# Products of masked scores and v in 64x64 tiles, a second copy of v, and another order of all steps

## The chip, the cores and the metric

The kernel runs on one core of one Trainium2 chip. The core has a matrix engine (TensorE, PE in the rows; PEld is its weight load), VectorE (DVE), ScalarE (ACT), GpSimd (POOL), and a sync engine (SP) whose queue issues all transfers. The metric is the device time of one execution in microseconds: before the change 369.61 us, the median of three runs (367.24 to 371.17).

## The reference

Inputs are q, k, v and f_logit of 4 batches, 8 heads, 768 positions and 48 channels. The first half is a gated linear recurrence for every head, the second a position mixing with a rotation and a channel mixing:

```python
f = 1.0 / (1.0 + np.exp(-f_logit))
for t in range(S):
    state = f[:, :, t, :, None] * state + np.einsum('bhd,bhe->bhde', k[:, :, t], v[:, :, t])
    y[:, :, t] = np.einsum('bhd,bhde->bhe', q[:, :, t], state)
x = y.transpose(0, 2, 1, 3).reshape(B, S, 384)
theta = x @ w_theta
zr, zi = x * np.cos(theta), x * np.sin(theta)
u = x + np.einsum('ts,bsd->btd', w_tok_r, zr) + np.einsum('ts,bsd->btd', w_tok_i, zi)
out = u + np.maximum(u @ w_ch, 0.0)
```

## The kernel before

The recurrence runs in 24 chunks of 128 positions, six for each batch. Gates become running sums of logarithms, q and k are scaled by them, and a chunk is then plain matrix work. q and k hold two heads in the partitions: of pair p (four of them) head 2p lies in rows 0 to 47 and head 2p+1 in rows 64 to 111. j is the head of the pair, t the half of the chunk (64 positions each).

The last chunk of a batch is taken whole (`whole_chunk`, 4 of 24). The other 20 go by halves, so that scores are needed only within a half:

- `sc` (L295): scores, k by q, 48 rows and 64 columns. The rows that a product reads follow from j, and its output lies in the rows of half t; the two heads write two PSUM banks.
- `ma` (L306): VectorE multiplies the scores by the causal mask, one instruction for each bank.
- `ke`, `kt`, `up` (L312, L324): k is turned and multiplied with v into the new state of either half; `sa`, `st`, `sm` add and fade the state.
- `ou` (L354, L361): L354 is the old state by q, and L361 the masked scores by v. The scores of one head lie in all 128 rows (half 0 above, half 1 below), so L361 loads 128 rows of weights, and v is kept with zeros in the rows of the other half: `vs[m]` has the two copies t = 0, 1, in two buffers `vz` that GpSimd fills with zeros at the start and mends after a whole chunk (L527).

A program matmul in fp32 takes two passes and stands as two MATMUL rows in the trace: L361 has 24 x 16 x 2 = 768.

After that `xc`, `xt`, `xs` bring the result to x and turn it, `th` (L405) are the angles, `tn`, `se`, `ab`, `tr`, `ro`, `zh`, `zl` the cosine, the sine and the split in two parts. `f` (L461) is one piece of the position mixing; there are 8 groups (batch and half of the output) of 18 pieces. `c` (L479) is the channel mixing, `cv` (L493) its end, and `so` the store.

The four engines run what the table `ORDER` names, in that order: each word is a step, taken the next time for the next chunk (or piece), and /A, /D or /P puts it on ScalarE, VectorE or GpSimd. SP's queue is issued in the order in which the loads become due in the same table (`lf`, `lk`, `lq`, `lv`; `lw` is a part of the weights, which arrive as 64-bit numbers and are decoded by `d1`, `d2`, `d3`). Of the pool `a`, which all of the recurrence uses, there are four PSUM banks.

Of the kernel before, what the change touches and what calls it, by code (L numbers as in the profile page):

```python
# [8 lines left out]
F32 = mybir.dt.float32  # L9
# [3 lines left out]
ALU = mybir.AluOpType  # L13
# [4 lines left out]
B, H, S, D = 4, 8, 768, 48  # L18
DM = H * D
P = 128  # L20
NP = H // 2
C = 128
NC = S // C
# [65 lines left out]
def gla_moe_kernel(  # L89
# [5 lines left out]
    v: bass.AP,  # L95
    vt: bass.AP,
# [6 lines left out]
    nc = tc.nc  # L103

    const = ctx.enter_context(tc.tile_pool(name="const", bufs=1))
    sb = ctx.enter_context(tc.tile_pool(name="sb", bufs=1))
# [25 lines left out]

    vz = [const.tile([P, 2, DM], F32, tag=f"v{i}", name=f"v{i}") for i in range(2)]
    for i in range(2):
        nc.gpsimd.memset(vz[i], 0.0)
# [95 lines left out]
    loaded, ps_, phased, vs = {}, {}, {}, {}  # L231
# [41 lines left out]

    pss, scs, psks, kts, pkvs, mids, states, pys, xs, pxts = ({} for _ in range(10))
    HALVES = [(t, slice(64 * t, 64 * t + 64)) for t in range(2)]

    def whole_chunk(m):
        return m % NC == NC - 1

    def bank(shape, name):  # L280
        return ps.tile(shape, F32, tag="a", bufs=4, name=name)

    def att_scores(m):
        kt, qt = loaded["k", m], loaded["q", m]
        pss[m] = [bank([P, NP, C], f"pss{m}{j}") for j in range(2)]
        for p in range(NP):
            if whole_chunk(m):
                for j in range(2):
                    r = slice(64 * j, 64 * j + D)
                    nc.tensor.matmul(pss[m][j][:, p, :], kt[r, p, :], qt[r, p, :], start=True, stop=True)  # L290
            else:
                for t, ts in HALVES:
                    for j in range(2):
                        r = slice(64 * j, 64 * j + D)
                        nc.tensor.matmul(pss[m][j][ts, p, :64], kt[r, p, ts], qt[r, p, ts], start=True, stop=True)  # L295

    def att_mask(m):
        if whole_chunk(m):
            w, mask = C, causal
            scs[m] = [sb.tile([P, NP, C], F32, tag="sc", bufs=2, name=f"sc{m}{j}") for j in range(2)]  # L300
        else:
            w, mask = C // 2, causal_h
            t = sb.tile([P, 2, NP, C // 2], F32, tag="sc", bufs=2, name=f"sc{m}")
            scs[m] = [t[:, j] for j in range(2)]
        for j in range(2):
            nc.vector.tensor_tensor(scs[m][j], pss[m][j][:, :, :w],  # L306
                                    mask.unsqueeze(1).to_broadcast([P, NP, w]), op=ALU.mult)
# [10 lines left out]
    def att_state(m):  # L318
        pkvs[m] = [bank([P, NP, D], f"pkv{m}{t}") for t in range(2)]
        for p in range(NP):  # L320
            for j, r in HALVES:
                h = 2 * p + j
                for t, ts in HALVES:
                    nc.tensor.matmul(pkvs[m][t][r, p, :], kts[m][ts, p, r], vs[m][ts, t, h * D:(h + 1) * D],  # L324
                                     start=True, stop=True)
# [16 lines left out]
    def att_out(m):  # L342
        qt, sc = loaded["q", m], scs[m]
# [13 lines left out]
        for p in range(NP):  # L357
            for j in range(2):
                h = 2 * p + j
                for t, ts in HALVES:  # L360
                    nc.tensor.matmul(pys[m][j][ts, p, :], sc[j][:, p, ts if whole_chunk(m) else slice(0, 64)],  # L361
                                     vs[m][:, 0 if whole_chunk(m) else t, h * D:(h + 1) * D],
                                     start=(old[t] is None and p == 0), stop=(p == NP - 1))
# [157 lines left out]
    def load_v(m):  # L521
        vs[m] = vz[m % 2]
        if whole_chunk(m):
            nc.sync.dma_start(vs[m][:, 0, :], v[m // NC, m % NC])
        else:
            if m > 1 and whole_chunk(m - 2):
                nc.gpsimd.memset(vs[m][64:, 0, :], 0.0)  # L527
            for t, ts in HALVES:
                nc.sync.dma_start(vs[m][ts, t, :], v[m // NC, m % NC, ts])
# [16 lines left out]
    def group(fn):  # L546
# [9 lines left out]
        "lv": load_v, "lw": load_part,  # L556
# [104 lines left out]
def layout(inputs):  # L661
    import numpy as np

    def rows(a):
# [11 lines left out]
        "v": np.ascontiguousarray(v.transpose(0, 2, 1, 3).reshape(B, NC, C, DM)),  # L676
        "vt": np.ascontiguousarray(vt),
# [25 lines left out]
```

## Time and profile before

| | |
|---|---|
| median of three runs | 369.61 us |
| the profiled execution | 370.48 us |
| its span | 368.7 us |
| mean granted clock of TensorE | 0.989 |
| PE busy | 341.1 us (93%) |
| DVE busy | 278.4 us (76%) |
| ACT busy | 195.0 us (53%) |
| POOL busy | 81.9 us (22%) |
| bytes moved | 40.82 MB |

The profile is of one execution. Its span goes from the first to the last instruction; the 1.8 us between the span and the execution's time lie outside the program's instructions. Busy times of one engine are unions, so instructions that overlap on one engine count once; mean durations are of single instructions. A row of the timeline merges neighbouring instructions of one line, and its second number reaches from the first start to the last end.

### The profile page before, as it was taken

The numbers are of one execution on the slowest core, as the hardware profiler recorded it, in microseconds if no ns is written. First come the engines' busy times: TensorE is split into PE (matmuls) and PEld (weight loads), VectorE is DVE, ScalarE is ACT, GpSimd is POOL, SyncE is SP. The second block draws the span as 40 slices with busy tenths as digits, with TensorE's granted clock in tenths as the row PEclk, the third lists the DMA queues.
The fourth block names the chain that finished last, engine by engine and source line by source line (L and its number), as shares of the span: only waits on it lengthen the run. The fifth ranks groups of instructions, "written<-read, shape, count | busy, mean of one in ns | idle before, by whom it ended". The sixth has DMA issues, their size and how long they took to land.

```text
span 368.7 us, 9853 instructions
## 1 busy us (share of the span) xinstructions
PE 341.1 (93%) x4176; PEld 295.3 (80%) x4176; DVE 278.4 (76%) x471; ACT 195.0 (53%) x326; POOL 81.9 (22%) x79
## 2 busy tenths in 40 slices
PE   0399799999998999999999999999999999999992
PEld 0386476655886679888999999989989999999992
DVE  4799998999779999998798997887775577304131
ACT  6599878554747938898856597346300335000000
POOL 4542610023832154651113430000100000000000
PEclk9999899999999999999999999999999999999997
DMA  7989789500443333324345432241100100010002
GB/s 264 349 279 349 229 260 331 170 2 15 125 148 109 108 92 80 98 75 128 97 134 151 129 98 58 73 115 30 34 23 23 44 0 2 21 43 2 22 23 92
DMA packets 21970, 40.82 MB, mean 111 GB/s; under 512 B 2720, under 2 KB 8864, under 8 KB 21920
## 3 DMA queue, kind: packets, MB, share of 16 engines
q1 hardware_dynamic: 21920, 40.12, 34.7%
q8 instruction: 35, 0.57, 0.7%
q14 instruction: 15, 0.12, 0.1%
HBM read 35.39 MB, written 4.72 MB: 109 GB/s over the span
## 4 chain that ended last, share of the span: by engine, by line
PE 64%; DVE 20%; DMA 6%; ACT 4%; issue 3%; POOL 1%; SPq 0%; DVEq 0%; ACTq 0%; POOLq 0%
PE pm L461 36%; PE pch L479 9%; PE pth L405 6%; PE py L361 3%; DVE f L249 3%; DVE k L269 2%; PE pss L295 2%; DMA f<-in_f_dram 2%; PE py L354 2%; PE pkv L324 2%; DMA raw<-in_w_i_dram 2%; PE psk L312 2%; DVE sc L306 1%; PE pxt L374 1%; DVE uhl L472 1%
## 5 line engine op out<-in xcount | busy, mean ns | idle before, releaser
L461 PE MATMUL pm<-wp,z 128*128 128x384 f32 x648 | 122.5, 340 | 0.0
L461 PEld LDWEIGHTS pm<-wp,z 128*128 128x128 f32 x648 | 111.6, 188 | 1.3
L461 PE MATMUL pm<-value,z 128*128 128x384 f32 x144 | 50.9, 501 | 0.4 <-DVE z L438 0.4
L479 PE MATMUL pch<-uhl,wch 128*128 128x384 f32 x216 | 41.9, 342 | 0.0
L461 PEld LDWEIGHTS pm<-value,z 128*128 128x128 f32 x144 | 26.7, 194 | 17.0 <-DVE z L438 0.8
L479 PEld LDWEIGHTS pch<-uhl,wch 128*128 128x128 f32 x216 | 37.1, 188 | 1.0 <-DVE ut L493 0.4
L249 DVE TENSOR_TENSOR_SCAN f<-carry,f 128x512 f32<-128x512 f32 x24 | 30.3, 1273 | 1.3 <-ACT f L245 1.3
L465 DVE TENSOR_TENSOR ut<-pm,ut 128x384 f32<-128x384 f32 x24 | 12.9, 553 | 23.6 <-PE pm L461 23.4
L239 POOL TENSOR_SCALAR f<-f 128x512 f32<-128x512 f32 x14 | 24.1, 1723 | 27.1 <-DMA f<-in_f_dram 23.9
L264 POOL TENSOR_TENSOR q<-q,p 128x512 f32<-128x512 f32 x15 | 22.5, 1500 | 29.4 <-DMA q<-in_q_dram 21.9
L260 POOL COPY pes<-p 128x4 f32<-128x4 f32 x24 | 10.9, 454 | 78.2 <-ACT p L256 78.1
L361 PE MATMUL py<-v,sc 128*64 128x48 f32 x768 | 28.1, 228 | 0.0
L256 ACT ACTIVATE p<-f 128x512 f32<-128x512 f32 x24 | 15.1, 630 | 23.4 <-DVE q L264 12.7
L295 PE MATMUL pss<-q,k 48*64 48x64 f32 x640 | 15.6, 234 | 12.7 <-DVE k L269 11.0
L146 ACT CAST uhl<-ut 128x384 fp32r<-128x384 f32 x14 | 6.9, 506 | 37.9 <-DVE ut L465 37.8
L361 PEld LDWEIGHTS py<-v,sc 128*64 128x64 f32 x768 | 25.1, 141 | 1.3
L493 DVE SCALAR_TENSOR_TENSOR ut<-pch,ut 128x384 f32<-128x384 f32 x24 | 13.2, 552 | 15.9 <-PE pch L479 15.8
L295 PEld LDWEIGHTS pss<-q,k 48*64 48x64 f32 x640 | 12.6, 142 | 15.6 <-DVE k L269 11.0
L405 PE MATMUL pth<-wth,xh 128*128 128x384 f32 x108 | 22.5, 343 | 1.0 <-DVE xh L146 0.8
L421 ACT ACTIVATE w<-w 128x384 f32<-128x384 f32 x22 | 11.5, 523 | 21.1 <-DVE w L416 21.1
L445 DVE TENSOR_TENSOR z<-w,z 128x768 fp32r<-128x768 f32 x18 | 18.3, 1019 | 4.2 <-ACT z L146 3.9
L324 PEld LDWEIGHTS pkv<-v,ktok 64*64 64x64 f32 x640 | 12.7, 142 | 10.2 <-issue 7.2
(87 smaller groups left out, 602.9 us busy)
## 6 DMA issues: line engine op xcount, KB each, us to landing
f<-in_f_dram SPq DMA_DIRECT2D x24, 256.0 KB, 2.8
q<-in_q_dram SPq DMA_DIRECT2D x24, 256.0 KB, 3.1
k<-in_k_dram SPq DMA_DIRECT2D x24, 256.0 KB, 3.4
raw<-in_w_r_dram SPq DMA_DIRECT2D x12, 384.0 KB, 5.0
raw<-in_w_i_dram SPq DMA_DIRECT2D x12, 384.0 KB, 5.6
out_dram<-ut SPq DMA_DIRECT2D x24, 192.0 KB, 2.0
v<-in_v_dram SPq DMA_DIRECT2D x40, 96.0 KB, 3.5
raw<-in_w_theta_dram SPq DMA_DIRECT2D x3, 384.0 KB, 5.8
```

Source lines behind the costliest of these rows:

```text
L239: on(nc.vector).tensor_scalar(ft, ft, F_MIN, None, op0=ALU.max)
L249: nc.vector.tensor_tensor_scan(fl, carry[:, pairs(h)].rearrange("p n t -> p (n t)"), fl, 0.0, ALU.mult, ALU.add)
L256: nc.scalar.activation(ps_[m][:, pairs(h)], ft, AF.Exp, scale=-1.0)
L264: on(nc.vector).tensor_tensor(qt, qt, ps_[m][:, pairs(h)], op=ALU.mult)
L295: nc.tensor.matmul(pss[m][j][ts, p, :64], kt[r, p, ts], qt[r, p, ts], start=True, stop=True)
L324: nc.tensor.matmul(pkvs[m][t][r, p, :], kts[m][ts, p, r], vs[m][ts, t, h * D:(h + 1) * D], start=True, stop=True)
L361: nc.tensor.matmul(pys[m][j][ts, p, :], sc[j][:, p, ts if whole_chunk(m) else slice(0, 64)], vs[m][:, 0 if whole_chunk(m) else t, h * D:(h ...
L405: nc.tensor.matmul(pths[m], l, r, start=(n == 0), stop=(n == len(ms) - 1))
L445: nc.vector.tensor_tensor(zs[m][:, 0], ws[m], zs[m][:, 1], op=ALU.subtract)
L461: nc.tensor.matmul(pms[g, d], l, r, start=(s == 0 and i == 0), stop=(s == NC - 1 and i == len(ms) - 1))
L479: nc.tensor.matmul(pcs[g, d], l, r, start=(es[0] == 0 and n == 0), stop=(es[-1] == KD - 1 and n == len(ms) - 1))
L493: nc.vector.scalar_tensor_tensor(u, pcs[g, d], 0.0, u, op0=ALU.max, op1=ALU.add)
```

## The change

The weights of L361 become 64 rows: the scores of head j are written to the rows of row tile j (both halves of the chunk side by side in the free dimension, one bank for both heads), the mask is applied in one instruction, and v comes a second time, by heads (`v_heads`, prepared outside the kernel), so that row tile j also holds v of head j for both halves. The state's update reads a plain copy of v. The buffers with zeros, their memsets and the two half loads go; a load `lz` comes in. In `ou` the loop over t is now outside the loop over j, in the whole chunks too. `ORDER` is written anew in all lines.

```diff
 ORDER = (
-    "lf lf lf lq gc lq go gc/P lq gc lk lk go gs lk lv go gs lv lw ge gs gq gp ge gk lw sc gk gq/P lf lf ke",
...
+    "lf lf lf lv lv gc/P lq lq gc/P gc go lq lz lz lk go gs lk lk go gs lw ge gs gq gp lw ge gk sc lf gk gq/P",
...
-    vz = [const.tile([P, 2, DM], F32, tag=f"v{i}", name=f"v{i}") for i in range(2)]
-    for i in range(2):
-        nc.gpsimd.memset(vz[i], 0.0)
...
     def att_scores(m):
         kt, qt = loaded["k", m], loaded["q", m]
-        pss[m] = [bank([P, NP, C], f"pss{m}{j}") for j in range(2)]
-        for p in range(NP):
-            if whole_chunk(m):
+        if whole_chunk(m):
+            pss[m] = [bank([P, NP, C], f"pss{m}{j}") for j in range(2)]
+            for p in range(NP):
                 for j in range(2):
                     r = slice(64 * j, 64 * j + D)
                     nc.tensor.matmul(pss[m][j][:, p, :], kt[r, p, :], qt[r, p, :], start=True, stop=True)
-            else:
+        else:
+            pss[m] = bank([P, NP, 2, 64], f"pss{m}")
+            for p in range(NP):
                 for t, ts in HALVES:
-                    for j in range(2):
+                    for j, js in HALVES:
                         r = slice(64 * j, 64 * j + D)
-                        nc.tensor.matmul(pss[m][j][ts, p, :64], kt[r, p, ts], qt[r, p, ts], start=True, stop=True)
+                        nc.tensor.matmul(pss[m][js, p, t, :], kt[r, p, ts], qt[r, p, ts], start=True, stop=True)
...
+            scs[m] = sb.tile([P, NP, 2, 64], F32, tag="sc", bufs=2, name=f"sc{m}")
+            nc.vector.tensor_tensor(scs[m].rearrange("s p t q -> s (p t) q"), pss[m].rearrange("s p t q -> s (p t) q"),
+                                    causal_h.unsqueeze(1).to_broadcast([P, 2 * NP, 64]), op=ALU.mult)
...
         for p in range(NP):
-            for j in range(2):
-                h = 2 * p + j
-                for t, ts in HALVES:
-                    nc.tensor.matmul(pys[m][j][ts, p, :], sc[j][:, p, ts if whole_chunk(m) else slice(0, 64)],
-                                     vs[m][:, 0 if whole_chunk(m) else t, h * D:(h + 1) * D],
-                                     start=(old[t] is None and p == 0), stop=(p == NP - 1))
+            for t, ts in HALVES:
+                for j, js in HALVES:
+                    if whole_chunk(m):
+                        h = 2 * p + j
+                        l, r = sc[j][:, p, ts], vs[m][:, h * D:(h + 1) * D]
+                    else:
+                        l, r = sc[js, p, t, :], vhs[m][js, t, p, :]
+                    nc.tensor.matmul(pys[m][j][ts, p, :], l, r, start=(old[t] is None and p == 0), stop=(p == NP - 1))
...
     def load_v(m):
-        vs[m] = vz[m % 2]
-        if whole_chunk(m):
-            nc.sync.dma_start(vs[m][:, 0, :], v[m // NC, m % NC])
-        else:
-            if m > 1 and whole_chunk(m - 2):
-                nc.gpsimd.memset(vs[m][64:, 0, :], 0.0)
-            for t, ts in HALVES:
-                nc.sync.dma_start(vs[m][ts, t, :], v[m // NC, m % NC, ts])
+        vs[m] = sb.tile([P, DM], F32, tag="v", bufs=2, name=f"v{m}")
+        nc.sync.dma_start(vs[m], v[m // NC, m % NC])
+
+    def load_vh(m):
+        vhs[m] = sb.tile([P, 2, NP, D], F32, tag="vh", bufs=2, name=f"vh{m}")
+        nc.sync.dma_start(vhs[m], v_heads[m // NC, m % NC])
```

Two places show how the built program's order moves. The first is TensorE in chunk 1, from the old state's products to the scores of chunk 2 (st0 and mid1 are the states of the two halves, py10 and py11 the outputs of the two heads, sc1 the masked scores). Before:

```order
L354 MATMUL py10_363<-st0_231,q1_107 64x48
L354 MATMUL py11_364<-st0_231,q1_107 64x48
L354 MATMUL py10_363<-mid1_358,q1_107 64x48
L354 MATMUL py11_364<-mid1_358,q1_107 64x48
...
L361 MATMUL py10_363<-v1_86,sc1_304 64x48 x2
L361 MATMUL py11_364<-v1_86,sc1_304 64x48 x2
...
L295 MATMUL pss20_412<-q2_113,k2_123 64x64
L295 MATMUL pss21_413<-q2_113,k2_123 64x64
```

And now:

```order
L352 MATMUL py10_355<-st0_235,q1_107 64x48
L352 MATMUL py11_356<-st0_235,q1_107 64x48
L352 MATMUL py10_355<-mid1_335,q1_107 64x48
L352 MATMUL py11_356<-mid1_335,q1_107 64x48
...
L363 MATMUL py10_355<-vh1_118,sc1_318 64x48
L363 MATMUL py11_356<-vh1_118,sc1_318 64x48
...
L295 MATMUL pss2_395<-q2_114,k2_127 64x64 x16
L322 MATMUL pkv20_428<-v2_285,ktok2_341 64x48
```

The products of scores and v now alternate between the heads as the old state's do, the 16 score products write one tile, and the state's update (L322) of chunk 2 follows them directly, where before a transposition stood between the two.

The second place is the start of SP's queue, from the third load of q to the first of the mixing weights (raw2; raw0 and raw1 are w_theta). Before:

```order
L518 DMA q2_113<-in_q_dram 128x512
L518 DMA k0_116<-in_k_dram 128x512
L518 DMA k1_118<-in_k_dram 128x512
L518 DMA k2_123<-in_k_dram 128x512
L172 DMA raw0_132<-in_w_theta_dram 128x768
L529 DMA v0_85<-in_v_dram 64x384 x2
L529 DMA v1_86<-in_v_dram 64x384 x2
L172 DMA raw0_132<-in_w_theta_dram 128x768
L172 DMA raw1_145<-in_w_theta_dram 128x768
L172 DMA raw2_180<-in_w_r_dram 128x768
```

And now:

```order
L518 DMA f2_98<-in_f_dram 128x512
L523 DMA v0_100<-in_v_dram 128x384
L523 DMA v1_102<-in_v_dram 128x384
L518 DMA q0_105<-in_q_dram 128x512
L518 DMA q1_107<-in_q_dram 128x512
L518 DMA q2_114<-in_q_dram 128x512
L527 DMA vh0_116<-in_v_heads_dram 128x384
L527 DMA vh1_118<-in_v_heads_dram 128x384
L518 DMA k0_120<-in_k_dram 128x512
L518 DMA k1_125<-in_k_dram 128x512
L518 DMA k2_127<-in_k_dram 128x512
L169 DMA raw0_132<-in_w_theta_dram 128x768 x2
```

The first k, which was the seventh transfer, is now the eleventh, behind two loads of v and two of its copy by heads.

## Rows read from the trace of the kernel before

**Rows 1.** Stretches: us, then PE, PEld, DVE, ACT, POOL busy, clock, DMA share, GB/s.

```profile
0.00:73.00 73.00, 54.82 (x815) 38.52 (x816) 62.55 (x98) 55.49 (x95) 23.66 (x29) 0.98 0.85 282
10.00:20.00 10.00, 5.15 (x86) 4.17 (x86) 7.62 (x13) 5.57 (x9) 6.03 (x5) 1.00 1.05 354
100.00:160.00 60.00, 58.32 (x886) 47.44 (x885) 56.34 (x88) 42.95 (x74) 27.13 (x21) 1.00 0.34 102
220.00:369.00 149.00, 141.93 (x1426) 137.26 (x1424) 83.10 (x158) 37.56 (x65) 2.27 (x4) 0.98 0.12 37
```

**Rows 2.** What TensorE waited for from 73 us on: total us, times, longest.

```profile
PE pth L405 <- DVE xh L146: 0.8, 1, 0.8
PE pkv L324 <- DMA v<-in_v_dram: 0.7, 1, 0.7
PE pkv L324 <- DVE sc L306: 0.4, 1, 0.4
...
PE pss L295 <- DVE w L416: 0.2, 1, 0.2
```

**Rows 3.** Timeline of TensorE at 73 us: start, us, engine, line, operation.

```profile
72.93 3.39 PE L461 MATMUL pm<-value,z 128*128 128x384 f32 x10
```

**Rows 4.** The chain of waits: its last piece, and one at 48 us.

```profile
48.83 6.50 DMA raw<-in_w_i_dram
...
361.97 0.56 DVE ut L493
```

**Rows 5.** Timeline of TensorE: merged bursts of L354 in one chunk, first and last.

```profile
255.65 0.23 PE L354 MATMUL py<-st,q 48*64 48x48 f32 x2
255.66 0.23 PE L354 MATMUL py<-mid,q 48*64 48x48 f32 x2
...
255.94 0.22 PE L354 MATMUL py<-st,q 48*64 48x48 f32 x2
```

**Rows 6.** Timeline of TensorE, 166 to 169 us: the products of a batch's first chunk.

```profile
166.65 0.67 PE L354 MATMUL py<-mid,q 48*64 48x48 f32 x16
167.24 1.14 PE L361 MATMUL py<-v,sc 128*64 128x48 f32 x32
168.31 0.69 PE L295 MATMUL pss<-q,k 48*64 48x64 f32 x32
168.94 0.45 PE L461 MATMUL pm<-wp,z 128*128 128x384 f32 x1
```

**Rows 7.** Timeline of TensorE, 192 to 194 us: scores and state's update back to back.

```profile
192.85 0.69 PE L295 MATMUL pss<-q,k 48*64 48x64 f32 x32
193.37 0.63 PE L324 MATMUL pkv<-v,ktok 64*64 64x48 f32 x32
```

**Rows 8.** Groups of VectorE: busy us, mean ns, idle before and its releaser.

```profile
L306 DVE TENSOR_TENSOR sc<-pss,causal_h 128x256 f32<-128x256 f32 x40 | 15.0, 416 | 4.7 <-PE pss L295 4.5
L306 DVE TENSOR_TENSOR sc<-pss,causal 128x512 f32<-128x512 f32 x8 | 5.1, 683 | 0.3 <-PE pss L290 0.3
L239 DVE TENSOR_SCALAR f<-f 128x512 f32<-128x512 f32 x10 | 6.7, 668 | 3.7 <-DMA f<-in_f_dram 3.6
L264 DVE TENSOR_TENSOR q<-q,p 128x512 f32<-128x512 f32 x9 | 6.1, 682 | 0.0
L185 DVE TENSOR_SCALAR raw<-raw 128x768 int32<-128x768 int32 (+1 forms) x16 | 9.2, 586 | 1.3 <-DMA raw<-in_w_theta_dram 1.3
L195 DVE SCALAR_TENSOR_TENSOR raw<-raw 128x768 int32<-128x768 int32 (+1 forms) x16 | 14.4, 901 | 0.0
L196 DVE SCALAR_TENSOR_TENSOR value<-raw 128x768 int32<-128x768 int32 (+1 forms) x14 | 14.0, 1000 | 0.5
```

**Rows 9.** Transfers: count, KB each, median us from issue to landing.

```profile
f<-in_f_dram SPq DMA_DIRECT2D x24, 256.0 KB, 2.8
raw<-in_w_r_dram SPq DMA_DIRECT2D x12, 384.0 KB, 5.0
v<-in_v_dram SPq DMA_DIRECT2D x4, 192.0 KB, 3.3
```

More of the change, by code (lines that the diff above doesn't have):

```diff
@@ L95, in gla_moe_kernel @@
     v: bass.AP,
+    v_heads: bass.AP,
     vt: bass.AP,
@@ L229, in gate_tables @@
             nc.scalar.preload_act_table_set(GATE_SET)
-    loaded, ps_, phased, vs = {}, {}, {}, {}
+    loaded, ps_, vs, vhs = {}, {}, {}, {}
     def pairs(h):
@@ L290, in att_scores @@
                     nc.tensor.matmul(pss[m][j][:, p, :], kt[r, p, :], qt[r, p, :], start=True, stop=True)
-            else:
+        else:
+            pss[m] = bank([P, NP, 2, 64], f"pss{m}")
+            for p in range(NP):
                 for t, ts in HALVES:
-                    for j in range(2):
+                    for j, js in HALVES:
                         r = slice(64 * j, 64 * j + D)
-                        nc.tensor.matmul(pss[m][j][ts, p, :64], kt[r, p, ts], qt[r, p, ts], start=True, stop=True)
+                        nc.tensor.matmul(pss[m][js, p, t, :], kt[r, p, ts], qt[r, p, ts], start=True, stop=True)
     def att_mask(m):
         if whole_chunk(m):
-            w, mask = C, causal
             scs[m] = [sb.tile([P, NP, C], F32, tag="sc", bufs=2, name=f"sc{m}{j}") for j in range(2)]
-        else:
-            w, mask = C // 2, causal_h
-            t = sb.tile([P, 2, NP, C // 2], F32, tag="sc", bufs=2, name=f"sc{m}")
-            scs[m] = [t[:, j] for j in range(2)]
-        for j in range(2):
-            nc.vector.tensor_tensor(scs[m][j], pss[m][j][:, :, :w],
-                                    mask.unsqueeze(1).to_broadcast([P, NP, w]), op=ALU.mult)
+            for j in range(2):
+                nc.vector.tensor_tensor(scs[m][j], pss[m][j], causal.unsqueeze(1).to_broadcast([P, NP, C]), op=ALU.mult)
+        else:
+            scs[m] = sb.tile([P, NP, 2, 64], F32, tag="sc", bufs=2, name=f"sc{m}")
+            nc.vector.tensor_tensor(scs[m].rearrange("s p t q -> s (p t) q"), pss[m].rearrange("s p t q -> s (p t) q"),
+                                    causal_h.unsqueeze(1).to_broadcast([P, 2 * NP, 64]), op=ALU.mult)
     def att_keys(m):
@@ L323, in att_state @@
                 for t, ts in HALVES:
-                    nc.tensor.matmul(pkvs[m][t][r, p, :], kts[m][ts, p, r], vs[m][ts, t, h * D:(h + 1) * D],
+                    nc.tensor.matmul(pkvs[m][t][r, p, :], kts[m][ts, p, r], vs[m][ts, h * D:(h + 1) * D],
                                      start=True, stop=True)
@@ L357, in att_out @@
         for p in range(NP):
-            for j in range(2):
-                h = 2 * p + j
-                for t, ts in HALVES:
-                    nc.tensor.matmul(pys[m][j][ts, p, :], sc[j][:, p, ts if whole_chunk(m) else slice(0, 64)],
-                                     vs[m][:, 0 if whole_chunk(m) else t, h * D:(h + 1) * D],
-                                     start=(old[t] is None and p == 0), stop=(p == NP - 1))
+            for t, ts in HALVES:
[6 more added lines that the diff above has]
+                    nc.tensor.matmul(pys[m][j][ts, p, :], l, r, start=(old[t] is None and p == 0), stop=(p == NP - 1))
     def att_x(m):
@@ L555, in gla_moe_kernel @@
     fn |= {
-        "lv": load_v, "lw": load_part,
+        "lv": load_v, "lz": inner(load_vh), "lw": load_part,
         "d1": decode_low, "d2": decode_high, "d3": decode_join, "d4": split_hi,
@@ L676, in layout @@
         "v": np.ascontiguousarray(v.transpose(0, 2, 1, 3).reshape(B, NC, C, DM)),
+        "v_heads": np.ascontiguousarray(v.reshape(B, NP, 2, NC, 2, 64, D).transpose(0, 3, 2, 5, 4, 1, 6)
+                                        .reshape(B, NC, P, 2, NP, D)),
         "vt": np.ascontiguousarray(vt),
```

66 rows, old and new, of the table ORDER are left out of this document.

## The prediction

> **What bounds the kernel now.** I read the busy time by stretch first. In the first 73 us [rows 1] VectorE is busy for 62.55 us, the transfers for 0.85 of the time at 282 GB/s, and TensorE for 54.82 us. After that TensorE is hardly ever idle: 58.32 of 60 us at 100 to 160 us, and in the last stretch all but the tail. The list of what TensorE waited for from 73 us on [rows 2] adds up to 2.6 us in six waits of 0.8 to 0.2 us. So there are two parts. The **front** ends where the tenth piece of the position mixing (f9) starts a run of such pieces, at 72.9 us [rows 3]; it is paced by VectorE and the transfers, and in places by both, since the chain of waits runs through a weight's landing of 6.50 us [rows 4]. The **rest**, 289 us up to the end of TensorE's work at 362.0 us [rows 4], goes at TensorE's own pace, and what lies there is worth what it costs TensorE. Counted from the two tables of steps, the blocks ahead of f9 are the same set before and after: chunks 0 to 5 with their angles, and nine pieces. So the rest holds the same blocks too, with 15 of the 20 chunks that go by halves.
>
> How long the small products take is read from the timeline. In the old state's products [rows 5] the rows come in bursts of four (two of st, two of mid: two heads by two halves, so four tiles of the array), and five bursts later, from 255.65 to 255.94 us, the clock has gone 0.29 us: a **round of 0.058 us**. A first chunk has only one half there, hence two tiles, and its 16 rows take 167.24 - 166.65 = 0.59 us [rows 6], as much as 32 rows in four tiles (scores, 168.94 - 168.31 = 0.63 us). The round stays at its length; what counts is how many different tiles it holds. L361 loads all 128 rows, so only the two halves of the columns are apart: 32 rows in 168.31 - 167.24 = 1.07 us.
>
> **The change part by part**, for the rest (15 chunks) where nothing else is said.
>
> *Products of scores and v.* With 64 rows of weights, alternating over heads and halves, they are in four tiles like the old state's: 8 rounds in place of 16, so 8 x 0.058 = 0.46 us less in a chunk, 7.0 us in 15.
>
> *Scores.* Their output now lies in the rows of their own head, so head 0 goes from row tile 0 to column tile 0 and head 1 from 1 to 1, for both halves. Two tiles of four are used, where before all four were. The nearest row is the first chunk's old state with two tiles [rows 6]: 16 rounds in place of 8, 0.46 us more in a chunk, **7.0 us in 15**. The two terms cancel. Bounds for the scores: no cost (four to a round as now), or single file (32 rounds, 1.9 us in place of 0.46). I take two to a round, since this alternation of two row tiles is the one that the row of 16 shows.
>
> *Changes of the tile's shape.* Scores followed directly by the state's update, both 64x64, start 193.37 - 192.85 = 0.52 us apart [rows 7]; scores followed by 128x128 work 0.63 us [rows 6]. A change of shape thus costs 0.11 us. Before, each `ou` goes from 64x64 to 128x64; now it stays, and often the next scores or update does too. Over both tables I count 134 changes of shape before and 93 after; in the rest 99 and 73. 26 x 0.11 = **2.9 us less**. Bounds: nothing, and 26 x 0.14 = 3.7 us (0.14 is L361's 1.07 less its 16 rounds).
>
> *Whole chunks.* In the products the column halves now come t0, t0, t1, t1 and no longer in turn. Neighbours in different tiles remain (second and third, fourth and next first), so I take nothing; the other end is one tile to a round in the three whole chunks of the rest: 3 x 16 x 0.058 = 2.8 us more.
>
> *Mask.* One instruction of 683 ns (the group of 128x512) for two of 416 [rows 8]: 0.15 us less of VectorE in a chunk, 2.2 us in 15. VectorE is busy 56.34 of 60 us at 100 to 160 us [rows 1], and it ended five of TensorE's six waits. Its relief can remove between none and all of the 2.6 us [rows 2]. I take **1.5 us less**. The memsets of GpSimd that go, and its clamps that come, have its idle time as cover (27 of 60 us busy at 100 to 160 us); if an order without slack had made q or f late, VectorE's queue would wait behind them.
>
> *Loads.* The copy of v by heads is 192 KB, as a whole load of v now [rows 9], for each of 20 chunks, 3.9 MB on 40.8. In the rest the transfers have room (0.34 of the time at 100 to 160 us [rows 1]), so it is hidden there; a load of v no longer waits for `ou` but only for the update. In the front it isn't free: up to the weight's part raw12, the last that is decoded ahead of f9, SP's queue holds 19392 KB against 17248 (27 loads of q, k and f against 25, 15 of v's 192 KB against 6.5; 3 + 22 of weights in both), so 2.2 MB more: 7.8 us at the front's 282 GB/s, 6.2 at 354, the most of any 10 us [rows 1].
>
> *VectorE in the front.* Ahead of f9 there are five masks (0.75 us), one clamp of 0.67 and one scaling of 0.68 fewer on it, one small instruction more, and one weight's decoding (0.59 + 0.90 + 1.00) is put behind f9 [rows 8]: about 4.2 us less of 62.55. The first chunk's chain also gets later, as its clamp goes to GpSimd and k0 stands behind four more loads, but its v is there earlier. Bounds for the start of f9: 4.2 us earlier if VectorE alone decides, 7.8 later if the transfers do. Nearer is VectorE's row, since its share of the front is the largest and chunk 5's inputs now stand ahead of the weights' second half in the queue; I take **1.0 us earlier**.
>
> *Sum.* Against the profiled execution of 370.5 us (span 368.7): -7.0 + 7.0 - 2.9 - 1.5 - 1.0 = -5.4, so 365.1. The median of the runs, 369.6, is 0.9 below that execution, so I predict **364.2 us**.
>
> **The rivals.**
>
> *A. The scores keep their pace* (8 %). If only the rows of the array had to differ, the two heads would suffice for a round of four, and the term of +7.0 falls away: 357.2 us. Against it stands the first chunk's row of 16 [rows 6], which has both heads and takes 0.59 us all the same. The Trainium skill (TensorE: Matmul & The Clock Gate, Part 3, The mechanism) says that a weight load overlaps running matmuls only when the row group differs, which by itself would give this rival's time; the trace disagrees with that as the whole rule, since L361's two products of a round share all 128 rows.
>
> *B. The new order gives it back* (18 %). All steps are placed anew, and a place that is right to a microsecond in one table can be wrong in the other. One more wait of VectorE or of a load of 4 to 5 us, like the landing on the chain [rows 4], and the result is 369 to 370 us. For it speaks that TensorE has only 2.6 us of waits left now; against it that VectorE has less to do.
>
> *C. The front becomes the transfers'* (9 %). Place: the loads up to raw12; price: 7.8 us at the rate of now. It decides from the point at which VectorE would reach that weight's decoding before it lands, some 65 us. Then f9 starts near 80 us, and 364.2 + 1.0 + 7.8 = 373.0 us, not quite 1 % slower, more if a change of shape costs less.
>
> *D. Two row tiles in one bank take turns* (5 %). Before, the two heads' scores went to two banks, in every row of the trace; now to one, so no row shows it. If they cannot write it together, a round holds one score product: 32 rounds in place of 16, 0.93 us more in each of 15 chunks, 13.9 us, and 378.1 us, slower by 2.3 %. The heads write different partitions, for which I give it little. The Trainium skill (TensorEngine Tiling (Array Packing), Restrictions and Gotchas, PSUM Pressure) says that different row tiles cannot access the same bank at one time, and names no exception for partitions; no run here shows it yet.
>
> **How the numbers follow.** The forecast has 60 %; its own range is 359 to 368.5 us, from the bounds of the front, the shape changes and the waits. To leave out no more than 2 in 10, the range runs from 358.5 (near A) to 371.5 (B whole, part of C). About 1 % is what a measurement of this kernel can tell from no change: 365.9 and 373.3 us. Two thirds of the forecast lie below 365.9, with A 0.50. C lies on the upper bound; half of it, D, and some combined mishaps of the order make 0.12 slower; 0.38 are left for the same.
>
> **What would show it.** L363's block (products of scores and v) near 0.5 to 0.6 us and the scores' near 1.0; if the scores stay at 0.6, A is right, at 2 D. The start of f9's run (72.9 before) tells the front: 69 to 74 for the forecast, 80 for C. From there to the end of TensorE's work I expect 284 to 286 us in place of 289. More than 5 us of TensorE's waits from f9 on would be B. The forecast is wrong if the front moves by over 4 us either way, or if the score blocks differ from 1.0 us.

## The result, and the profile after

The changed kernel takes **365.58 us** (median of 20 runs, 363.24 to 367.8), the kernel before 371.11 us on the same chip (20 runs, 367.24 to 375.32). The ratio is **0.9876, with a 95% interval of 0.9849 to 0.9903**: faster by 1.2%, 364.2 us against 369.6 having been predicted (a ratio of 0.985). Ratios leave out runs more than 1.5% above the fastest of their kernel (2 of the 20 before, and 2 of the 4 in the first experiment), so they aren't the quotients of the medians beside them. The total was near; its two parts were not.

| profiled execution, us | before | after | difference | predicted |
|---|---|---|---|---|
| time / span | 370.48 / 368.7 | 367.22 / 365.5 | -3.3 / -3.2 | -5.4 |
| front: start of f9's run | 72.93 | 76.36 | **+3.4** | -1.0 |
| rest: from there to the end of TensorE's work | 289.0 | 282.2 | **-6.8** | -4.4 |

The profiled execution of before is 0.6 us below its median and that of after 1.6 above, so the table shows 3.3 us of the medians' 5.5, and the +3.4 of the front is that of one execution each; another kernel of the new order, with only the mask split (below), starts f9 at 75.97.

**The rest.** Two stretches of the profile after (columns as in [rows 1]) answer to those of before, and below them stands everything that TensorE waited for from 70 us on, which answers to [rows 2].

```profile
100.00:160.00 60.00, 60.00 (x936) 50.03 (x932) 53.14 (x85) 46.90 (x80) 21.75 (x19) 1.00 0.42 127
220.00:366.00 146.00, 138.51 (x1388) 134.54 (x1386) 85.05 (x156) 39.97 (x72) 3.45 (x6) 0.99 0.13 42
```

```profile
PE pm L461 <- DVE ut L465: 0.5, 1, 0.5
```

TensorE is now busy 60.00 of 60 us, and one wait of 0.5 us is left of 2.6. VectorE went from 56.34 to 53.14 us there. What the small blocks cost is seen in TensorE's timeline, as in [rows 6] and [rows 7] (start, us, engine, line, operation):

```profile
157.84 0.68 PE L352 MATMUL py<-st,q 48*64 48x48 f32 x32
158.46 1.17 PE L363 MATMUL py<-v,sc 128*64 128x48 f32 x32
159.56 1.15 PE L295 MATMUL pss<-q,k 48*64 48x64 f32 x32
160.64 1.31 PE L461 MATMUL pm<-wp,z 128*128 128x384 f32 x6
...
173.24 0.65 PE L363 MATMUL py<-vh,sc 64*64 64x48 f32 x32
173.71 1.12 PE L295 MATMUL pss<-q,k 48*64 48x64 f32 x32
174.77 0.44 PE L461 MATMUL pm<-wp,z 128*128 128x384 f32 x1
```

From start to start, the products with v of a half chunk take 173.71 - 173.24 = **0.47 us** (1.07 in [rows 6]), the scores 174.77 - 173.71 = **1.06** and 1.08 at 159.56 (0.63 before). The whole chunk's products take 159.56 - 158.46 = 1.10, against 1.07 for the half-loaded products of before: the other order of its loops costs nothing that can be seen.

Adding up, for every product of the rest, the time from its start to the next one's (idle time apart) gives the account of the 6.8 us:

| TensorE in the rest, us | before | after | difference |
|---|---|---|---|
| products with v, L361 / L363 | 19.23 | 11.07 | -8.2 |
| scores of half chunks, L295 | 8.90 | 15.77 | +6.9 |
| old state, L354 / L352 | 11.10 | 9.12 | -2.0 |
| whole chunks' scores, state's update | 12.47 | 12.48 | 0.0 |
| idle | 2.67 | 0.54 | -2.1 |
| position mixing's packed weights (wp) | 117.67 | 116.34 | -1.3 |
| all other work | 116.95 | 116.84 | -0.1 |

The change of tile shape between two products falls on the earlier one. From start to start, the last old-state product of a chunk took 0.148 us when L361 with another shape followed, and 0.039 when L363 with the same shape does: 0.11 us, so the 15 such changes that are gone make 1.6 of the 2.0 us. A product with packed weights (wp) takes 0.268 us when a smaller tile follows and 0.173 (the median) when its own shape does; 17 of them stood before such a change and 9 do now, which is 0.8 of their 1.3 us. I count 101 changes in the rest before and 75 after, 62 and 40 of them behind small products.

The mask's groups on VectorE (columns as in [rows 8]) show the one instruction in place of two:

```profile
L304 DVE TENSOR_TENSOR sc<-pss,causal_h 128x512 f32<-128x512 f32 x20 | 13.7, 687 | 9.9 <-PE pss L295 9.7
L301 DVE TENSOR_TENSOR sc<-pss,causal 128x512 f32<-128x512 f32 x8 | 5.1, 684 | 0.4 <-PE pss L288 0.4
```

**The front.** It ends later although VectorE is busy for less of it, 58.74 us of 73 against 62.55 [rows 1]. The chain of waits of after (start, us, what), to be read against [rows 4]:

```profile
46.69 0.97 DVE value L193
...
47.67 0.33 SPq L169
...
48.05 5.33 DMA raw<-in_w_i_dram
...
53.47 0.56 DVE raw L182
...
57.60 0.69 DVE sc L301
58.34 1.10 PE py L352 x30
59.44 1.91 PE py L363 x32
61.34 3.55 PE pm L461 x8
```

A weight's load waits for a buffer, which VectorE's decoding of an earlier weight sets free (L193, to 47.66 us); SP issues it at once; it lands at 53.4 us; and VectorE, which has come to that weight's decoding in its queue, has stood for it. The same load before, in the timeline of SP:

```profile
36.27 0.42 SPq L172 DMA_DIRECT2D raw<-in_w_i_dram  x1
```

This weight part (raw8) landed at 42.1 us before, the last one ahead of f9 (raw12) at 62.2 and now at 71.1. The transfers and their durations are not what changed (columns as in [rows 9]; v's copy is the new row):

```profile
raw<-in_w_r_dram SPq DMA_DIRECT2D x12, 384.0 KB, 4.5
raw<-in_w_i_dram SPq DMA_DIRECT2D x12, 384.0 KB, 5.4
...
vh<-in_v_heads_dram SPq DMA_DIRECT2D x20, 192.0 KB, 3.6
```

The loads are issued later: raw8's second one at 48.05 us, where it was at 36.27 before, and the mixing weights are asked for later from the third of them on (26.41 against 16.20 us; 1.5 us for the fourth, 6 to 12 for all that follow). Behind the weight stand the step that fades the state on VectorE (mid) and the products that need it; TensorE's timeline and the stretches around it:

```profile
54.35 0.26 PE L352 MATMUL py<-mid,q 48*64 48x48 f32 x2 [2.04 <-DVE mid L330]
...
59.37 1.98 PE L363 MATMUL py<-v,sc 128*64 128x48 f32 x32
61.27 3.62 PE L461 MATMUL pm<-value,z 128*128 128x384 f32 x8
...
66.99 2.75 PE L461 MATMUL pm<-value,z 128*128 128x384 f32 x8
...
76.36 2.10 PE L461 MATMUL pm<-value,z 128*128 128x384 f32 x6
```

```profile
0.00:73.00 73.00, 51.98 (x804) 38.74 (x805) 58.74 (x85) 52.09 (x89) 24.24 (x28) 0.93 0.85 282
52.00:54.00 2.00, 0.32 (x18) 0.19 (x10) 1.07 (x3) 1.97 (x4) 0.00 (x0) 1.00 0.98 322
54.00:56.00 2.00, 1.65 (x70) 1.60 (x72) 1.79 (x5) 1.97 (x5) 0.00 (x0) 1.00 0.91 289
56.00:58.00 2.00, 1.22 (x14) 0.93 (x10) 1.97 (x4) 2.00 (x3) 1.23 (x1) 0.51 0.95 324
60.00:62.00 2.00, 2.00 (x27) 1.69 (x25) 1.97 (x3) 1.06 (x3) 0.00 (x0) 0.50 1.02 375
62.00:64.00 2.00, 2.00 (x6) 1.18 (x5) 1.76 (x3) 0.46 (x1) 0.00 (x0) 0.78 0.78 174
```

TensorE stands still for 2.04 us, up to 54.35. From 56 us its granted clock is at 0.5, the lower of the two levels (1.2 GHz), and back at 1.00 (2.4 GHz) between 62 and 64 us. From 58.34 on the chain runs through TensorE itself, so there the lower clock counts in full: L352's 30 products took 1.10 against 0.68 at 157.84 us, L363's whole chunk 1.98 against 1.17, and the first piece of the mixing 3.62 against 2.75. Together this is 2.1 us; with the wait of 2.04 it is more than the whole +3.4, so other parts of the front must have come earlier. The mean clock of the first 73 us fell from 0.98 to 0.93.

### The profile page after: what moved, and what is told of

It reads as the page before. It is cut to its first block, busy times and chain, and to the rows that moved or that the text cites. A ratio compares the mean times of both kernels' runs of the same rounds, so it can differ in the third digit from the quotient of the medians.

```text
span 365.5 us, 9814 instructions
## 1 busy us (share of the span) xinstructions
PE 336.9 (92%) x4176; PEld 295.0 (81%) x4176; DVE 276.9 (76%) x438; ACT 198.8 (54%) x337; POOL 85.6 (23%) x80
## 4 chain that ended last, share of the span: by engine, by line
PE 80%; DVE 8%; DMA 6%; issue 2%; ACT 1%; SPq 1%; DVEq 0%; ACTq 0%
PE pm L461 40%; PE pch L479 10%; PE pth L405 10%; PE pss L295 5%; PE py L363 4%; PE py L352 4%; DMA raw<-in_w_i_dram 3%; PE pkv L322 3%; PE psk L310 3%; DVE raw L192 2%; PE pxt L374 2%; DMA raw<-in_w_theta_dram 2%; ACT raw L187 1%; DMA q<-in_q_dram 1%; DVE raw L182 1%
## 5 line engine op out<-in xcount | busy, mean ns | idle before, releaser
L236 POOL TENSOR_SCALAR f<-f 128x512 f32<-128x512 f32 x19 | 30.4, 1603 | 37.7 <-DMA f<-in_f_dram 26.4
L295 PE MATMUL pss<-q,k 48*64 48x64 f32 x640 | 26.0, 233 | 11.8 <-DVE k L266 11.8
L295 PEld LDWEIGHTS pss<-q,k 48*64 48x64 f32 x640 | 23.7, 146 | 12.3 <-DVE k L266 11.8
L261 POOL TENSOR_TENSOR q<-q,p 128x512 f32<-128x512 f32 x16 | 23.8, 1486 | 37.9 <-DMA q<-in_q_dram 35.3
L143 ACT COPY x<-py 128x192 f32<-128x192 f32 x42 | 11.2, 319 | 36.5 <-PE py L363 36.5
L257 POOL COPY pes<-p 128x4 f32<-128x4 f32 x24 | 9.7, 404 | 59.3 <-ACT p L253 59.3
L438 DVE TENSOR_TENSOR w<-w,x 128x768 f32<-128x768 f32 x18 | 20.3, 1125 | 3.8 <-ACT w L429 3.7
L304 DVE TENSOR_TENSOR sc<-pss,causal_h 128x512 f32<-128x512 f32 x20 | 13.7, 687 | 9.9 <-PE pss L295 9.7
```

The lines of the kernel that those rows point to most:

```text
L143: (nc.scalar.copy if on(usual) is nc.scalar else on(usual).tensor_copy)(dst, src)
L236: on(nc.vector).tensor_scalar(ft, ft, F_MIN, None, op0=ALU.max)
L261: on(nc.vector).tensor_tensor(qt, qt, ps_[m][:, pairs(h)], op=ALU.mult)
L295: nc.tensor.matmul(pss[m][js, p, t, :], kt[r, p, ts], qt[r, p, ts], start=True, stop=True)
L438: nc.vector.tensor_tensor(zs[m] if full else w, w, xs[m].unsqueeze(1).to_broadcast([P, 2, DM]), op=ALU.mult)
```

## The experiments

All "before" times are of runs of the kernel before on the same chip as the experiment. The edits are shortened: names, start and stop flags, rearrangements and unchanged lines between are left out.

**Four tiles for the scores.** Scores of head j in odd pairs go to the other row tile, so that four neighbours are in four tiles again; this takes one bank for each head and two masks of 128x256.

```diff
-pss[m] = bank([P, NP, 2, 64])
+pss[m] = [bank([P, 2, 2, 64]) for j in range(2)]
-  nc.tensor.matmul(pss[m][js, p, t, :], kt[r, p, ts], qt[r, p, ts])
+  p, js = 2 * g + o, HALVES[j ^ o][1]
+  nc.tensor.matmul(pss[m][j][js, g, t, :], kt[r, p, ts], qt[r, p, ts])
```

> The changed kernel, but head j of every second pair writes its scores to the rows of the other row tile, in two banks (by head), so that four score products in a row are in four different tiles; the mask is two instructions of 128x256 again. The products with v read the scores as if they still lay by head, so the output is not the reference's; the amount of work is the same. Theory 1 (a round of 0.058 us holds as many products as there are different tiles): the score block falls from 1.08 to 0.61-0.63 us in all 20 half chunks, f9 to the end of TensorE's work from 282.2 to about 282.2 - 15 x 0.46 = 275.3 us, the whole kernel about 7 us faster than the changed one (some 358), less if VectorE's second mask instruction (0.15 us a chunk) brings waits back. Rival (the rows of the array alone decide, or the 64 columns that are loaded): the block stays at 1.08 and the time at 365.

368.85 us (4 runs, 363.26 to 371.12) against 369.16, ratio 0.990 (0.979 to 1.000). The blocks did get short. TensorE's timeline of this kernel, one block without a wait and one behind it:

```profile
94.83 0.69 PE L296 MATMUL pss<-q,k 48*64 48x64 f32 x32
95.46 1.56 PE L463 MATMUL pm<-value,z 128*128 128x384 f32 x4
...
109.82 0.69 PE L296 MATMUL pss<-q,k 48*64 48x64 f32 x30 [1.19 <-DVE xl L398]
110.44 1.56 PE L463 MATMUL pm<-value,z 128*128 128x384 f32 x4
```

The block takes 95.46 - 94.83 = 0.63 us, as before the change.

Its list of what TensorE waited for from 70 us on, however, has

```profile
PE pss L296 <- ACT x L143: 3.1, 4, 1.8
PE pss L296 <- DVE xl L398: 3.1, 2, 1.9
PE pss L296 <- DVE ut L143: 0.8, 1, 0.8
```

All of these are scores that wait for a bank: the new order is laid out for one bank of them, and the second must be waited for. Idle time in the rest is 8.0 us, and the rest 289.6. The profile is of the longest of the four runs, so the others may have waited less. f9 starts at 73.94 us here, which the part on the front comes back to. The part on the tiles stood, the time did not.

**Two banks, the same two tiles.** Head 0's scores in one bank, head 1's in another, for rival D and for the question whether the shared bank or the two tiles make a block take 1.08 us.

```diff
-pss[m] = bank([P, NP, 2, 64])
+pss[m] = [bank([P, NP, 2, 64]) for j in range(2)]
-  nc.tensor.matmul(pss[m][js, p, t, :], kt[r, p, ts], qt[r, p, ts])
+  nc.tensor.matmul(pss[m][j][js, p, t, :], kt[r, p, ts], qt[r, p, ts])
```

> The changed kernel, but the two heads' scores go to two banks as before the change, still in the tiles (0,0) and (1,1); the mask is two instructions on 64 partitions each. Theory 1 (number of different tiles): the score block stays at 1.08 us. Rival (two row tiles in one bank take turns): the block falls to 0.63 us. The whole time says little, as the masks cost VectorE about 0.69 us more in each chunk.

One run, 381.34 us, with 7.6 us of waits in the rest, most of them the same waits for a bank (its masks, on 64 partitions, are also two of 687 ns). The time says little; the timeline says what was asked:

```profile
229.79 1.11 PE L295 MATMUL pss<-q,k 48*64 48x64 f32 x30 [0.55 <-DVE xl L398]
230.83 1.31 PE L463 MATMUL pm<-wp,z 128*128 128x384 f32 x6
```

The last 30 of 32 products take 1.04 us with two banks too. Sharing a bank costs nothing; two tiles in place of four cost the 0.45 us.

**The new products in the old order.** The order of before, with v's second load right behind its first.

```diff
-d1 lk up d2 gs ke lv d2 th lw
+d1 lk up d2 gs ke lv lz d2 th lw
```

> The new products and loads, in the order of steps from before the change; the load of v by heads stands right behind each load of v. Theory 1: score block 1.08, products with v 0.47, from f9 to the end 289.0 less 20 changes of shape (99 to 79) x 0.11 = 286.8 us, so the new products alone are worth 2 us there, and the front comes later by some part of the 2 MB more; total 369 to 371 against 371.1 before. Rival (the products bring all of the gain and the order nothing): about 366.

365.64 us (4 runs) against 369.16, ratio 0.989 (0.983 to 0.994): as fast as the whole change, which I had not expected. f9 starts at 73.70 us, raw8 and raw12 land at 43.4 and 63.0, nearly as before. The rest is 284.5 us, 4.5 less than before: the small products -2.8, idle -1.55. So the products bring the gain, and the loads of v's copy, in these places, moved the front by 0.8 us.

**The old products in the new order.** The converse, without v's second load.

```diff
-lv lz d2 th lw
+lv d2 th lw
```

> The old products and loads, in the order of steps of the changed kernel without the load of v by heads. Theory 1: TensorE's changes of shape from f9 on are 100, as before (99), so the rest gains only what VectorE's relief gives (its waits, 2.6 us, and its copies and casts moved off), and the front is as with the change but for the 1.5 to 2 MB less: 367 to 369 us. Rival (the new order needs the new products: two banks for scores make its steps wait): slower than 371.

394.85 us (4 runs), ratio 1.071 (1.062 to 1.080); f9 starts at 84.8 us. What TensorE waited for most in this kernel, beside the first k at its start:

```profile
PE py L363 <- DMA v<-in_v_dram: 11.7, 8, 2.5
```

The order loads the next v into a buffer that the old products have still to read, so they wait for a load that isn't theirs, and the output is not the reference's. The order can't be had without the products, and this run doesn't give its price with them.

**The two orders joined.** The new products; up to f9 the old order with v's second load as above, from f9 on the new order (steps that one part had already done are left out of the other).

```diff
 ... lw d3 ab/A tr     (old order up to here)
-f tn d1 d4 se f ro    (old)
+f d4 f tn f d2 se ro  (new)
```

> The changed kernel with the old order up to the tenth mixing piece (f9), the load of v by heads right behind each load of v, and the changed order from there on. Theory 1 (the products' gain is TensorE's and lies behind f9; the new order loses 2.7 us ahead of f9 and gains 2.3 behind it): f9 starts near 73.7 as in the old order, and the rest takes 282.2 as in the changed kernel, so about 2.7 us faster than the changed one, some 362.5 to 363.5. Rival (the late front has left work done that the rest then profits from): the rest takes 284 to 285 and the time stays at 365.

**362.36 us** (6 runs, 360.91 to 363.56) against 369.21, ratio **0.981 (0.977 to 0.985)**: faster than the kernel before. Against the changed one it is 3.2 us by the medians, and 0.7% or 2.4 us by the two ratios, whose intervals just touch; they were not timed side by side. The changed kernel with its mask split, timed beside it, took 365.99 (below), its fastest run 364.65 against the slowest of 363.56 here. Its stretches and its start of f9:

```profile
50.00:60.00 10.00, 8.93 (x132) 6.09 (x132) 9.34 (x14) 8.75 (x15) 1.48 (x1) 1.00 0.98 334
60.00:70.00 10.00, 10.00 (x95) 6.40 (x93) 9.90 (x15) 6.27 (x13) 0.00 (x0) 1.00 0.87 287
100.00:160.00 60.00, 60.00 (x936) 50.54 (x928) 52.76 (x84) 49.75 (x85) 19.91 (x17) 1.00 0.40 130
```

```profile
72.80 1.45 PE L463 MATMUL pm<-value,z 128*128 128x384 f32 x4
```

The front is that of before again, at the full clock through 50 to 70 us (0.9 us earlier than in the third experiment, whose steps up to f9 are the same: that much is the spread of single executions, and covers the third's 0.8). From f9 on TensorE has no wait at all, and the rest is 280.6 us.

**v's copy by heads only for the first two chunks.** Eighteen loads of 192 KB left out, in the new order.

```diff
+if m < 2:
     vhs[m] = sb.tile([P, 2, NP, D]); dma_start(vhs[m], v_heads[...])
+else:
+    vhs[m] = vhs[m % 2]
```

> The changed kernel, but v by heads is loaded for the first two chunks alone and used again by all others, so 18 loads of 192 KB are left out and the output is not the reference's. Theory 1 (the front is late because the new order puts the weights behind the inputs, not because of the bytes): raw12 lands at 67 to 70 in place of 71.1 and f9 starts at 75 to 76 (76.4 with the change). Rival C of the prediction (the bytes make the front): f9 starts near 73 and the time falls by 3 us or more.

364.48 us (8 runs), ratio 0.988 (0.984 to 0.992); f9 starts at 74.73, raw8 lands at 51.4 and raw12 at 69.8. SP's timeline (start, us of issue):

```profile
47.40 0.33 SPq L169 DMA_DIRECT2D raw<-in_w_r_dram  x1
47.78 0.42 SPq L169 DMA_DIRECT2D raw<-in_w_i_dram  x1
```

raw8's second load is issued at 47.78 us, 0.27 earlier than with the copies, and lands 3.65 us later in place of 5.33. f9 is 1.6 us earlier than after the change, but in this execution TensorE's lower clock also lasts only from 58.8 to 62.2 us, 3.4 us in place of 6.9, so how much of it is the bytes' isn't shown; against the kernel before, the time is the same as with all copies (ratios 0.988). That the weights are asked for some 11 us later than before is the order's doing.

**The mask split in two.** Two of 128x256 in place of one of 128x512, the rest as changed.

```diff
+for g in (slice(0, 2), slice(2, 4)):
-    nc.vector.tensor_tensor(scs[m], pss[m], causal_h)
+    nc.vector.tensor_tensor(scs[m][:, g], pss[m][:, g], causal_h)
```

> The changed kernel with the mask in two instructions of 128x256 in place of one of 128x512, so 0.15 us more of VectorE in each of 20 chunks, nothing else. Theory 1 (VectorE's relief took TensorE's waits away): 0.5 to 1.5 us of the 2.1 us of waits come back, 366 to 367. Rival (VectorE has room, the waits went with the freed bank or with the order): no change, 365.6.

365.99 us (7 runs), ratio 0.990 (0.987 to 0.994); the rest 282.0 us with 0.5 us of waits, as after the change. The mask's relief of VectorE isn't what took the waits away.

**Four tiles in the old order, the sum on VectorE.** The scores as in the first experiment; the products with v of odd pairs then land in the other head's bank, and VectorE adds them (two of 128x96 for a chunk).

```diff
-nc.tensor.matmul(pys[m][j][ts, p, :], l, r)
+dst = pys[m][j][ts, p, :] if p % 2 == 0 else pys[m][1 - j][ts, NP + p // 2, :]
+nc.tensor.matmul(dst, l, r)
+nc.vector.tensor_tensor(xv[:, 1::2, j, :], pys[m][1 - j][:, NP:, :], xv[:, 1::2, j, :], op=ALU.add)
```

> The old order with the new products, but head j of every second pair writes its scores to the rows of the other row tile (four tiles in a round, two banks by head), its products with v go to the bank of that row tile, and VectorE adds the two parts of x (two instructions of 128x96 for each chunk); v by heads is laid out for it. Theory 1: the score block is 0.61 us, 15 x 0.46 = 6.9 us less of TensorE behind f9 than in the old order with the new products (284.5); VectorE has some 0.7 us more a chunk, and between none and all of the gain is lost in waits for it: 360 to 367. Rival (VectorE or the banks decide behind f9 as soon as TensorE is relieved): no faster than 365.6.

369.64 us (10 runs), ratio 0.999 (0.996 to 1.003). TensorE's timeline and its largest waits from 76 us on:

```profile
193.54 0.69 PE L298 MATMUL pss<-q,k 48*64 48x64 f32 x32
194.05 0.63 PE L326 MATMUL pkv<-v,ktok 64*64 64x48 f32 x32
```

```profile
PE pxt L397 <- DVE x L390: 2.3, 2, 1.7
PE pkv L326 <- DVE sc L308: 1.0, 1, 1.0
```

The scores' block, 194.05 - 193.54 = 0.51 us, has all four tiles, and the scores of the rest take 9.27 us in place of 15.52. Against this the rest has 5.2 us of waits, mostly for VectorE, and f9 starts at 76.4 us. Of TensorE's saving of 6.3 us, the waits give back 4.1 (1.1 us of idle time with two tiles), and the late front 2.7.

**Two banks for the halves, in the old order.** For the rest of the waits: one bank for the scores of each half, two masks.

```diff
-pss[m] = bank([P, NP, 2, 64])
+pss[m] = [bank([P, NP, 64]) for t in range(2)]
-  nc.tensor.matmul(pss[m][js, p, t, :], kt[r, p, ts], qt[r, p, ts])
+  nc.tensor.matmul(pss[m][t][js, p, :], kt[r, p, ts], qt[r, p, ts])
```

> The old order with the new products, but the scores of the two halves go to two banks, each masked by an instruction of 128x256; still two tiles in a round. It differs from the old order with the new products by one more bank held from scores to mask, and by the mask in two instructions, which e7 has shown to cost nothing behind f9. Theory 1 (the freed bank took part of TensorE's waits away): from f9 on the waits rise from 1.1 us back towards the 2.7 of before, and the rest takes 285.5 to 286.5 in place of 284.5. Rival (the bank decides nothing in this order): 284.5, and the time stays at 365.6.

367.12 us (10 runs) against 370.08, ratio 0.993 (0.989 to 0.998). The rest is 283.6 us with 0.6 of waits, no longer than with one bank (284.5 and 1.1); f9 starts at 75.5 us, behind 4.6 us in which scores wait for a bank ahead of it. In the old order the free bank decides nothing behind f9. My theory, that one bank less took the waits away, falls for this order.

## Why the prediction was right, and where it was wrong

The forecast's branch is what happened, and the result lies in its own range. Two of its own signs did not come: f9 at 69 to 74 us (76.36) and the rest at 284 to 286 (282.2). Its terms:

- **Products of scores and v, -7.0**: right. 0.47 us for a block; the -8.2 of the rest are 1.2 more than the rounds make, and 12 fewer changes of shape stand behind these blocks (6 in place of 18).
- **Scores, +7.0**: right, +6.9. The one row of 16 in [rows 6] was the right neighbour. Rival A (0.6 us a block) falls: with both heads and two tiles a block takes 1.06 to 1.08 us, and with four tiles 0.51 when the next work has the same shape (eighth experiment). Rival D (turns in one bank) falls too: two products went to a round, with one bank or with two. The Trainium skill (TensorEngine Tiling (Array Packing), Restrictions and Gotchas, PSUM Pressure) bars different row tiles from one bank at a time. The trace doesn't agree for tiles that write different partitions: 1.06 us here, where the prediction put turns at 1.9.
- **Changes of shape, -2.9**: right. Of the 26 fewer, 22 stand behind small products at 0.11 us and 4 behind 128x128 work at 0.095, the prices read above: -2.8 us. The small products together give -8.2 + 6.9 - 2.0 = -3.3 us, and the rounds of the first two cancel; so 0.9 us is more than their 22 changes make, and its cause is open.
- **Whole chunks, 0**: right, 1.10 against 1.07 us.
- **TensorE's waits, -1.5**: the size was near, -2.1, the reason was wrong. I had the mask's relief of VectorE remove them; with the mask split again they stay away. With the products in the old order 1.1 us are left, in the joined order none. What removes them (fewer loads of v that wait for `ou`, the places of the steps, or chance) stays open.
- **Position mixing, not named in the sum: -1.3 us.** Its packed weights take 117.66 us in the old order with the new products and 116.18 in the joined one, so it comes with the new order. Of it 0.8 us are changes of shape behind these products (9 in place of 17), a part of the term above; what else there is was not isolated.
- **Front, -1.0**: this step failed; it measured +3.4. I weighed bytes (up to +7.8) against VectorE's work (down to -4.2), took VectorE's row as the nearer since its share of the front was larger, and set the order's part to nothing. VectorE's work in the first 73 us did fall, by 3.8 (in part since its later work now comes after that), and it didn't help: the front is a loop in which a load waits for a buffer, the buffer for the decoding of an earlier weight, and the decoding for its place in VectorE's queue. The new order puts these places later. That loop is read from the chain; no run moved one decoding alone. The runs part the +3.4 as follows: the same loads in the old order up to f9 cost -0.1 and 0.8 us in two executions (72.80 and 73.70); without the copies the new order still starts f9 at 74.73, 1.8 later than before. Three runs blur this. The old order with a second bank starts f9 at 75.5 (ninth) and 76.4 (eighth), with 4.6 and 3.4 us of scores waiting for a bank before it; and the new order with four tiles for the scores and all loads starts it at 73.94, so shorter scores, or the spread of single executions, can give most of the +3.4 back. That 2.1 us of it are the lower clock behind a wait of 2.04 us is worked out from the rows of after; no run changed the clock by itself. Such a stretch of 3.4 to 6.9 us between 56 and 65 us is in all five traces of the new products in the new order, and in none of the five traces of the old order up to f9.
- **Rival B** (the order gives it back) was right in its mechanism for the front, at 3.4 us and not at the 4 to 5 that would have undone the gain; in the rest the new order brought 3.9 us (284.5 with the old, 280.6 in the joined one). **Rival C** had the place, not the cause: raw12 came at 71 us, but for the queue's order and not for the rate, which stayed at 282 GB/s. What the copies' bytes add is 1.6 us at most in the executions compared, and not 7.8.

So the two parts erred in opposite ways, the front by 4.4 us and the rest by 2.4, and the sum came out 2 us too low for the profiled execution: that the total was near is in part luck. The gain comes from the tiles only indirectly: what the products save the scores give back, and what remains is fewer changes of shape and fewer waits.

## What to carry to other kernels

Small products ran in rounds here that hold as many as there are different tiles next to each other in the queue; a layout that gives one product four tiles by taking two from another gains nothing in itself, so count tiles on both sides of the intermediate. In a front where loads, decodings and buffers form a loop, read for each weight when its load is *issued* and what set its buffer free; shares of busy time don't tell whether a new order asks for it later. A change that mixes a new operation with a new order of all steps is taken apart by giving each the other's half, and here joining the better half of each order beat both.

## What the runs showed of the hardware

- A change of tile shape cost TensorE about 0.1 us: 0.268 us from a packed-weight product to a smaller tile against 0.173 to its own shape, 0.148 against 0.038 us behind the last of a block of small products, and a score block of 0.51 us before the state's update (same shape) against 0.63 before 128x128 work.
- Two row tiles that write different partitions of one PSUM bank ran two to a round of 0.058 us (32 products in 1.06 us); with a bank for each the last 30 took 1.04 us.
- TensorE, busy 0.32 of 2 us at 52 to 54 us and 1.65 of 2 at 54 to 56, went to the lower clock at 56 us for some 7 us, in which blocks took 1.3 to 1.7 times as long (3.62 against 2.75 us, 1.98 against 1.17), 2.1 us together. That its wait of 2.04 us brought the lower clock isn't shown: in the eighth experiment TensorE stood for the whole of 58 to 60 us, and the granted clock stayed at 1.00 there and up to the kernel's tail (a stretch as in [rows 1]).

```profile
58.00:60.00 2.00, 0.00 (x0) 0.00 (x0) 0.31 (x1) 1.13 (x2) 0.00 (x0) 1.00 0.98 373
```
